# Loading the values and output weights of a decode kernel's full-cache part from Pool's software DMA queue

## The chip, the cores, the metric

One Trainium2 chip, one core. The time is the device time of one execution in microseconds (us), as the median of several executions. "Span" is the length of the one profiled execution, which is 1.7 to 1.9 us shorter than its time. PE is the matmul engine (TensorE), DVE is VectorE, ACT ScalarE, Pool GpSimd, SP SyncE.

## The reference

Two attention decode steps, their outputs side by side: part A has a sliding window and 4 query heads per key head, part B has 32 heads over a full cache of 8192 positions. Batch 4, one query position, bfloat16.

```python
def _B_ref(x, k_cache, v_cache, wq, wo):           # A: the last 2048 positions, 8 key heads
    B, Sq, D = x.shape                             # 4, 1, 512
    H, Dh = 32, 128
    q = (x @ wq).reshape(B, Sq, H, Dh).transpose(0, 2, 1, 3)
    scores = jnp.einsum("bhqd,bhkd->bhqk", q, k_cache) * (Dh ** -0.5)
    p = softmax(scores)
    o = jnp.einsum("bhqk,bhkd->bhqd", p, v_cache)
    return o.transpose(0, 2, 1, 3).reshape(B, Sq, H * Dh) @ wo
return jnp.concatenate([a, b], axis=-1)
```

The caches of B alone are 2 x 268 MB, each byte used once. It is a kernel of loads.

## The kernel before

Part B is cut into 64 chunks: two heads of one batch element each. A chunk has 4 MB of keys and 4 MB of values (128 partitions, one row of 32 KB in each). On PE, the keys are transposed tile by tile and multiplied with the query ("keys"); the values of the chunk before are multiplied with its probabilities in between ("values"). Two buffers of keys and two of values; every fourth chunk 256 KB of output weights, in one buffer. I call the chunks of B 0 to 63.

All loads are issued by SP, in one line, in the order of their use: keys c+1, values c, keys c+2, ...

```python
def dma_wos(hp):                                   # output weights, waits until their reader is done
    src = B_wo[2 * hp * P:2 * (hp + 1) * P, :].rearrange("(p r) n -> p (r n)", r=2)
    sch.add_dma("sp", lambda e: e.dma_start(wos[...], src), "d_wos",
                waits=[("fin", NCA + 4 * hp - 1)] if hp else [], key=("wos", hp))

def dma_kv(kind, c):
    ...                                            # waits: the last reader of the buffer (transposes or products)
    if kind == "v" and c == NC - 1:                # last values: five pieces, 64, 32, 16, 8, 8 tiles
        for i, n in enumerate(LASTV):
            sch.add_dma("sp", lambda e, x=x: e.dma_start(dst[:, x], src[:, x]), "d_vl%d" % i, ...)
        return
    if kind == "k" and c == NC - 1:                # last keys: 96 tiles (24 KB rows), then 32 (8 KB rows)
        sch.add_dma("sp", lambda e: e.dma_start(dst[:, x[0]], src[:, x[0]]), "d_h%d" % at, ...)
        sch.add_dma("sp", lambda e: e.dma_start(dst[:, x[1]], src[:, x[1]]), "d_kl", key="kl")
        return
    sch.add_dma("sp", lambda e: e.dma_start(dst, src), "d_h%d" % at, waits=waits, key=(kind, c))

for kind, c in loads:                              # k0 k1 v0 k2 v1 ...
    if kind == "k" and c >= NCA and (c == NCA or (c - NCA) % 4 == 3 and c > NCA + 3):
        dma_wos((c - NCA) // 4)
    dma_kv(kind, c)
    ...
```

On PE, for each chunk c: `keys_part(c)`, 16 groups of 8 transposes and 8 score products, then `values_part(c - 1, c)`.

Of the kernel before, what the change touches and what calls it, by code (L numbers as in the profile page):

```python
# [11 lines left out]

P = 128
TG = 8
NTRB = 3
NKT = 4
NH = 10
NWO = 3
# [141 lines left out]
def bass_concat_heads__sliding_block_cached__mha_block_cached__decode_kernel(  # L160
# [30 lines left out]
    NC = len(chunks)  # L191
    NCA = Hkv
    groups = []
    for c, ch in enumerate(chunks):
        ch["UC"] = ch["U"] * ch["C"]
        assert ch["NT"] % TG == 0 and ch["NT"] * P * 2 <= (1 if ch["ab"] == 0 else 2) * 16384
        ch["NG"] = ch["NT"] // TG
        ch["s"] = len(groups)
# [5 lines left out]
    NONE = -1  # L204
    sch = _Sched()
    with ExitStack() as es:
        block = es.enter_context(nc.Block())

        def sb(name, shape, dt):
            return es.enter_context(nc.sbuf_tensor(name, shape, dt))  # L210

        def ps(name, shape, dt):
            return es.enter_context(nc.psum_tensor(name, shape, dt))

        kv = sb("kv", [P, NH, 8192], BF16)
        kt = sb("kt", [P, NKT, TG * P], BF16)
        wos = sb("wos", [P, 2, DO], BF16)
# [31 lines left out]
        wol = sb("wol", [P, 2, DO], BF16)  # L249
        tr = ps("tr", [P, NTRB, TG * P], BF16)  # L250
        sc = ps("sc", [P, 2, 512], F32)
        po = ps("po", [P, 512], F32)
        ms = ps("ms", [P, 512], F32)
        fin = ps("fin", [P, 512], F32)
        xtps = ms[:, XT0:XT0 + KC * NB].bitcast(BF16)

        semnames = ["eng_pe", "eng_dve", "eng_act", "eng_pool", "eng_sp", "d_x0", "d_x1", "d_o0", "d_o1"]
        semnames += ["d_h%d" % i for i in range(NH)] + ["d_vl%d" % i for i in range(len(LASTV))]
        semnames += ["d_wo%d" % i for i in range(NWO)] + ["d_wos", "d_kl"]
        sems = {n: es.enter_context(nc.semaphore(n)) for n in semnames}  # L260


# [42 lines left out]
        def take(load, at, n, release):  # L305
            waits = []
            for i in range(at, at + n):
                waits += held[i]
                held[i] = [release]
            half_of[load] = at  # L310
            return waits

        def flat(at, n):
            return kv[:, at:at + n, :].rearrange("p s x -> p (s x)")
# [10 lines left out]
        def wo_slot(g):  # L325
            return g % 2 if g < NCA - 1 else 2

        def dma_wo(g):

            src = A_wo[g * 4 * P:(g + 1) * 4 * P, :].rearrange("(p r) n -> p (r n)", r=4)  # L330
            slot = wo_slot(g)
            dst = wor[:, slot, :]
            sch.add_dma("sp", lambda e: e.dma_start(dst, src), "d_wo%d" % slot,
                        waits=[("fin", g - 2)] if g >= 2 and slot < 2 else [], key=("wo", g))

        def dma_wos(hp):


            src = B_wo[2 * hp * P:2 * (hp + 1) * P, :].rearrange("(p r) n -> p (r n)", r=2)
            sch.add_dma("sp", lambda e: e.dma_start(wos[:, :, :].rearrange("p r n -> p (r n)"), src), "d_wos",  # L340
                        waits=[("fin", NCA + 4 * hp - 1)] if hp else [], key=("wos", hp))

        def dma_kv(kind, c):
            ch = chunks[c]
            T = {("k", 0): A_k, ("k", 1): B_k, ("v", 0): A_v, ("v", 1): B_v}[(kind, ch["ab"])]

            at = HALF_A[kind][c % 2] if ch["ab"] == 0 else (0 if kind == "k" else 4) + 2 * (c % 2)

            if kind == "v" and c == NC - 1:
                at = 8  # L350
            waits = take((kind, c), at, 1 if ch["ab"] == 0 else 2, ("T", ch["s_last"]) if kind == "k" else ("pv", c))
            if kind == "v" and c == NCA + 1:
                waits = waits + [("pv", NONE)]
            if ch["ab"] == 0:
                src = T[:, ch["g"], SkA - W:, :].rearrange("b (pp j) d -> pp b (j d)", pp=P // NB)
                sch.add_dma("sp", lambda e: e.dma_start(kv[:, at, :], src), "d_h%d" % at, waits=waits, key=(kind, c))
                return
            src = T[ch["b"], 2 * ch["hp"]:2 * ch["hp"] + 2].rearrange("u (pp j) d -> (u pp) (j d)", pp=P // 2)
            dst = flat(at, 2)
            if kind == "v" and c == NC - 1:  # L360

                j0 = 0
                for i, n in enumerate(LASTV):
                    x = slice(j0 * P, (j0 + n) * P)
                    sch.add_dma("sp", lambda e, x=x: e.dma_start(dst[:, x], src[:, x]), "d_vl%d" % i, waits=waits, key=("vl", j0))  # L365
                    j0 += n
                return
            if kind == "k" and c == NC - 1:

                x = slice(0, LASTK * P), slice(LASTK * P, NTB * P)  # L370
                sch.add_dma("sp", lambda e: e.dma_start(dst[:, x[0]], src[:, x[0]]), "d_h%d" % at, waits=waits, key=(kind, c))
                sch.add_dma("sp", lambda e: e.dma_start(dst[:, x[1]], src[:, x[1]]), "d_kl", key="kl")
                return
            sch.add_dma("sp", lambda e: e.dma_start(dst, src), "d_h%d" % at, waits=waits, key=(kind, c))

        dma_x(0)
        dma_x(1)
# [7 lines left out]
        loads.remove(("v", NCA - 1))  # L385
        loads.insert(loads.index(("k", NCA)), ("v", NCA - 1))
        for kind, c in loads:
            if kind == "k" and c >= NCA and (c == NCA or (c - NCA) % 4 == 3 and c > NCA + 3):
                dma_wos((c - NCA) // 4)
            dma_kv(kind, c)  # L390
            if kind == "v" and c > NCA and (c - NCA) % 2 == 1:


                hp = max(0, c - NCA - 2) // 4
                sch.add("sp", lambda e: e.sem_inc(sems["eng_sp"], 1), waits=[("wos", hp)] + (["kl"] if c == NC - 1 else []),
                        key=("wos2", c - 2 if c > NCA + 1 else NONE), self_inc=True)
            if kind == "v" and c < NCA:
                dma_wo(c)
        sch.add("sp", lambda e: e.sem_inc(sems["eng_sp"], 1), waits=[("wos", HB // 2 - 1)], key=("wos2", NC - 1), self_inc=True)


# [4 lines left out]
        def pe_mm(o, l, r, start=True, stop=True, transpose=False, waits=(), key=None):  # L406
            if transpose:
                sch.add("pe", lambda e: e.transpose(o, l, r), waits, key)  # L408
            else:
                sch.add("pe", lambda e: e.matmul(o, l, r, start=start, stop=stop), waits, key)  # L410
# [41 lines left out]
        def ahead(c, n):  # L452

            return c - n if c - n >= NCA else NONE

        bank_used = [None] * NTRB

        def emit_T(s):
            c, g = groups[s]
            bank = g % NTRB  # L460
            if c == NCA and g == 0:
                bank_used[:] = [None] * NTRB
            before, bank_used[bank] = bank_used[bank], s
            for t in range(TG):
                waits = []
                if t == 0:
                    waits = [("k", c), "c_identb"] if g == 0 else []
                    waits += [("ev", before)] if before is not None else []
                    if c >= NCA and c % 2 == 1 and g == LASTK // TG:
                        waits += [("wos2", ahead(c, 2))]  # L470
                pe_mm(tr[:, bank, t * P:(t + 1) * P], tile_of("k", c, g * TG + t), identb[:, :], transpose=True,
                      waits=waits, key=("T", s) if t == TG - 1 else None)
            src, dst = tr[:, bank, :], kt[:, s % NKT, :]
            waits = [("T", s)] + ([("S", s - NKT)] if s >= NKT else [])
            if (g % 3 == 2) if c >= NCA else (g in (0, 1, 3, 5)):
                sch.add("act", lambda e: e.activation(dst, src, ACTF.Copy), waits=waits, key=("ev", s))  # L476
            else:
                sch.add("dve", lambda e: e.tensor_copy(dst, src), waits=waits, key=("ev", s))  # L478
# [268 lines left out]
        def keys_part(c):  # L747
            ch = chunks[c]
            if c % 2 == 0:
                sch.mark()  # L750
            for g in range(ch["NG"]):
                emit_T(ch["s"] + g)
                if g >= SLAG:
                    emit_S(ch["s"] + g - SLAG)

                for what in A_ORDER.get(g, []) if c < NCA else []:
                    do_A(what, c)
                if c >= NCA and c % 2 == 0 and g == 6:
                    norm_sum(ahead(c, 1))
                if c >= NCA and c % 2 == 1 and g == 8:  # L760
                    emit_sel(ahead(c, 2))
                if c >= NCA and c % 2 == 1 and g == 10:
                    emit_fin(ahead(c, 2))
# [117 lines left out]
```

## Time and profile before

| | before |
|---|---|
| time, median | 1374.2 us |
| bytes read | 587.2 MB, 428 GB/s over the span |
| DMA engines, share of the span in packets | 99.8% |
| PE busy | 86% |
| last landing, then to the end of the span | 1369.1 us, 3.5 us |

The page has one digit per fortieth of the span for each engine (tenths of busy time), and a GB/s row below. A load's "us to landing" counts from its issue, so it includes the wait behind earlier loads of its queue. The lines stand in the prediction.

### The profile page before, as it was taken

How to read it: one execution, taken by the hardware profiler on the slowest of the kernel's cores; microseconds unless marked ns; L12 is line 12 of the kernel's file. 1: busy time of each engine (PE TensorE's matmuls, PEld its weight loads, DVE VectorE, ACT ScalarE, POOL GpSimd, SP SyncE). 2: the span in 40 equal slices, each digit the busy share in tenths (PEclk: the TensorE clock that was granted, in tenths of full speed). 3: DMA queues.
4: the chain of work that ended last, by engine and by line, in shares of the span. 5: the costliest groups of instructions: out<-in, count | busy, mean ns of one | idle time of the engine just before them, and what ended most of it. 6: DMA issues, size and time to landing. Idle time of an engine off the chain costs nothing.

```text
span 1372.6 us, 59967 instructions
## 1 busy us (share of the span) xinstructions
PE 1176.5 (86%) x27065; PEld 1132.9 (83%) x27067; DVE 656.6 (48%) x1434; ACT 434.7 (32%) x650; POOL 7.3 (1%) x28
## 2 busy tenths in 40 slices
PE   4888898889888888988888888888898888888888
PEld 4777898888888888888888878888898888888888
DVE  1775454445444444454445444444454444444544
ACT  1553232333223322332233323322333233323322
POOL 2000000000000000000000000000000000000000
PEclk9998999999999999999999999999999999999999
DMA  9999999999999999999999999999999999999998
GB/s 400 423 424 432 429 433 428 433 432 432 432 431 433 429 434 428 434 430 434 430 434 430 430 433 432 432 431 433 429 433 431 434 429 434 430 432 432 432 427 352
DMA packets 25261, 587.53 MB, mean 428 GB/s; under 512 B 2820, under 2 KB 2840, under 8 KB 6296
## 3 DMA queue, kind: packets, MB, share of 16 engines
q1 hardware_dynamic: 25208, 587.22, 99.8%
q8 instruction: 16, 0.26, 0.1%
q14 instruction: 5, 0.04, 0.0%
q10 hardware_dynamic: 32, 0.01, 0.0%
HBM read 587.21 MB, written 0.01 MB: 428 GB/s over the span
## 4 chain that ended last, share of the span: by engine, by line
DMA 65%; PE 33%; issue 1%; DVE 1%; ACT 0%; SPq 0%; DVEq 0%
DMA kv<-in_B_k_cache_dram 57%; PE tr L408 21%; PE sc L410 9%; DMA kv<-in_A_k_cache_dram 5%; DMA kv<-in_B_v_cache_dram 3%; PE po L410 2%; PE fin L410 1%; PE ms L410 0%; ACT kt L476 0%; DVE sA L527 0%; SPq L365 0%; ACT pba L597 0%; PE ms L408 0%; DVE zA L683 0%; DVE rm L536 0%
## 5 line engine op out<-in xcount | busy, mean ns | idle before, releaser
L408 PE MATMUL tr<-identb,kv 128*128 128x128 bf16 x8704 | 697.9, 230 | 148.8 <-DMA kv<-in_B_k_cache_dram 141.5
L478 DVE COPY kt<-tr 128x1024 bf16<-128x1024 bf16 x736 | 502.6, 690 | 457.1 <-PE tr L408 452.7
L408 PEld LDWEIGHTS tr<-identb,kv 128*128 128x128 bf16 x8704 | 552.9, 104 | 165.2 <-DMA kv<-in_B_k_cache_dram 81.7
L476 ACT ACTIVATE kt<-tr 128x1024 bf16<-128x1024 bf16 x352 | 359.3, 1023 | 666.8 <-PE tr L408 666.7
L410 PE MATMUL sc<-qb,kt 128*128 128x64 bf16 x8704 | 446.2, 196 | 14.3 <-ACT kt L476 12.8
L410 PEld LDWEIGHTS sc<-qb,kt 128*128 128x128 bf16 x8704 | 366.4, 100 | 26.0 <-ACT kt L476 20.2
L410 PE MATMUL po<-pbb,kv 128*128 128x64 bf16 x8320 | 284.4, 192 | 4.5 <-issue 3.9
L410 PEld LDWEIGHTS po<-pbb,kv 128*128 128x128 bf16 x8320 | 263.2, 97 | 7.1 <-issue 4.1
L577 ACT ACTIVATE pbb<-sc,negb 64x128 bf16<-64x128 f32 x128 | 51.6, 403 | 254.3 <-DVE negb L564 253.5
L541 DVE TENSOR_REDUCE rm<-sc 64x1 f32<-64x128 f32 x128 | 37.0, 289 | 56.6 <-PE sc L410 55.7
L553 DVE TENSOR_REDUCE gm<-ms 1x2 f32<-1x128 f32 (+1 forms) x72 | 20.1, 279 | 48.4 <-PE ms L408 48.4
L564 DVE COPY negb<-ms 128x1 f32<-128x1 f32 (+1 forms) x72 | 11.4, 158 | 47.0 <-PE ms L410 46.8
L410 PE MATMUL ms<-identf,gx 1*128 1x1 f32 (+1 forms) x144 | 27.2, 256 | 0.8 <-DVE zA L683 0.8
L666 DVE TENSOR_TENSOR oz<-po,rz 128x8 bf16<-128x8 f32 x33 | 5.5, 166 | 40.7 <-PE po L410 40.7
L410 PEld LDWEIGHTS ms<-identf,gx 1*128 1x128 f32 (+1 forms) x144 | 21.1, 182 | 4.6 <-DVE zA L683 0.9
L577 ACT ACTIVATION_READ_ACCUMULATOR pbb<-sc,negb 64x1 f32 x128 | 23.7, 185 | 0.0
L410 PE MATMUL po<-pba,kv 128*128 128x64 bf16 x512 | 20.5, 199 | 3.5 <-issue 2.1
L410 PEld LDWEIGHTS po<-pba,kv 128*128 128x128 bf16 x512 | 17.9, 102 | 5.7 <-ACT pba L597 4.2
L408 PE MATMUL ms<-identf,rm 128*1 128x128 f32 (+1 forms) x72 | 19.5, 271 | 2.4 <-DVE rm L536 2.3
L557 DVE TENSOR_SCALAR gx<-gm 1x128 f32<-1x128 f32 (+1 forms) x72 | 16.0, 222 | 2.5
L683 DVE CAST zB<-ms 64x8 bf16<-64x8 f32 x64 | 10.5, 164 | 9.2 <-PE ms L410 8.7
L410 PE MATMUL ms<-xT,kv 128*128 128x4 bf16 x256 | 7.1, 166 | 8.8 <-DMA kv<-in_A_wq_dram 5.0
(61 smaller groups left out, 173.9 us busy)
## 6 DMA issues: line engine op xcount, KB each, us to landing
kv<-in_B_k_cache_dram SPq DMA_DIRECT2D x63, 4096.0 KB, 26.5
kv<-in_B_v_cache_dram SPq DMA_DIRECT2D x63, 4096.0 KB, 30.9
kv<-in_A_k_cache_dram SPq DMA_DIRECT2D x8, 2048.0 KB, 14.8
kv<-in_A_v_cache_dram SPq DMA_DIRECT2D x8, 2048.0 KB, 16.2
kv<-in_A_wq_dram SPq DMA_DIRECT2D x1, 4096.0 KB, 12.5
kv<-in_B_wq_dram SPq DMA_DIRECT2D x1, 4096.0 KB, 27.1
wor<-in_A_wo_dram SPq DMA_DIRECT2D x8, 512.0 KB, 9.8
wos<-in_B_wo_dram SPq DMA_DIRECT2D x16, 256.0 KB, 20.3
```

Of the source, the lines that this page charges most:

```text
L408: sch.add("pe", lambda e: e.transpose(o, l, r), waits, key)
L410: sch.add("pe", lambda e: e.matmul(o, l, r, start=start, stop=stop), waits, key)
L476: sch.add("act", lambda e: e.activation(dst, src, ACTF.Copy), waits=waits, key=("ev", s))
L478: sch.add("dve", lambda e: e.tensor_copy(dst, src), waits=waits, key=("ev", s))
L541: sch.add("dve", lambda e, src=src, pp=pp: e.tensor_reduce(out=rm[pp, m, 0:1], in_=src, axis=AX.X, op=ALU.max), waits=[("S", ch["s_last"]) ...
L553: sch.add("dve", lambda e: e.tensor_reduce(out=gm[0:C, m, 0:U], in_=src, axis=AX.X, op=ALU.max), waits=[("trm", c)], key=("gmax", c))
L557: sch.add("dve", lambda e: e.tensor_scalar(out=dst, in0=gv, scalar1=-scale, scalar2=None, op0=ALU.mult), waits=[("gmax", c)], key=("gx", c))
L564: sch.add("dve", lambda e: e.tensor_copy(negb[:, m, 0:C], ms[:, col:col + C]), waits=[("bc", c)], key=("negb", c))
L577: sch.add("act", lambda e, src=src, pp=pp, n=n, u=u: e.activation(probs_of(c)[pp, :, u], src, ACTF.Exp, bias=negb[pp, m, 0:1], scale=scale ...
L666: sch.add("dve", lambda e: e.tensor_tensor(out=o, in0=i0, in1=i1, op=ALU.mult), waits=waits, key=("oT", c))
L683: sch.add("dve", lambda e, src=src, pp=pp: e.tensor_copy(z[pp, :].rearrange("p (r b) -> p r b", r=k), src), waits=[("sm", c)] + free if h ...
```

## The change

Intent: take the values and the output weights off SP's line, so that keys and values, whose buffers come free at different moments, wait apart and not in one line. Pool had nothing to do after the first 10 us.

```diff
+VQ = "pool"
 ...
 def dma_wo(g):                                    # sliding part
+    if slot == 2:
+        sch.add_dma(VQ, lambda e: e.dma_start(dst, src), "d_p6", waits=[("k", g)], key=("wo", g))
+        return
 ...
 def dma_wos(hp):
-    sch.add_dma("sp", ..., "d_wos",
+    sch.add_dma(VQ if hp else "sp", ..., "d_ws" if hp else "d_wos",
                 waits=[("fin", NCA + 4 * hp - 1)] if hp else [], key=("wos", hp))
 ...
+    if kind == "v" and c == NCA:                  # the first values: after ten groups of the first keys
+        waits = waits + [("T", ch["s"] + 10)]
 ...
-            sch.add_dma("sp", lambda e, x=x: e.dma_start(dst[:, x], src[:, x]), "d_vl%d" % i, ...)
+            sch.add_dma(VQ, lambda e, x=x: e.dma_start(dst[:, x], src[:, x]), "d_vl%d" % i, ...)
 ...
-    sch.add_dma("sp", lambda e: e.dma_start(dst, src), "d_h%d" % at, waits=waits, key=(kind, c))
+    sch.add_dma("sp" if kind == "k" else VQ, lambda e: e.dma_start(dst, src),
+                ("d_h%d" if kind == "k" else "d_p%d") % at, waits=waits, key=(kind, c))
+
+def dma_values(c):                                # the order on Pool
+    if c > NCA + 3 and (c - NCA) % 4 == 1:
+        dma_wos((c - NCA) // 4)
+    dma_kv("v", c)
```

(Cut: SP's signal that the weights have landed moves behind the keys; new semaphores; the lines that call `dma_values` among PE's instructions, eleven groups into a chunk's keys, two in the last chunk.)

More of the change, by code (lines that the diff above doesn't have):

```diff
@@ L258, in bass_concat_heads__sliding_block_cached__mha_block_cached__decode_kernel @@
         semnames += ["d_h%d" % i for i in range(NH)] + ["d_vl%d" % i for i in range(len(LASTV))]
-        semnames += ["d_wo%d" % i for i in range(NWO)] + ["d_wos", "d_kl"]
+        semnames += ["d_wo%d" % i for i in range(NWO)] + ["d_wos", "d_kl", "d_ws", "d_p4", "d_p6"]
         sems = {n: es.enter_context(nc.semaphore(n)) for n in semnames}
@@ L332, in dma_wo @@
             dst = wor[:, slot, :]
+            if slot == 2:
+                sch.add_dma(VQ, lambda e: e.dma_start(dst, src), "d_p6", waits=[("k", g)], key=("wo", g))
+                return
             sch.add_dma("sp", lambda e: e.dma_start(dst, src), "d_wo%d" % slot,
-                        waits=[("fin", g - 2)] if g >= 2 and slot < 2 else [], key=("wo", g))
+                        waits=[("fin", g - 2)] if g >= 2 else [], key=("wo", g))
         def dma_wos(hp):
             src = B_wo[2 * hp * P:2 * (hp + 1) * P, :].rearrange("(p r) n -> p (r n)", r=2)
-            sch.add_dma("sp", lambda e: e.dma_start(wos[:, :, :].rearrange("p r n -> p (r n)"), src), "d_wos",
+            sch.add_dma(VQ if hp else "sp", lambda e: e.dma_start(wos[:, :, :].rearrange("p r n -> p (r n)"), src), "d_ws" if hp else "d_wos",
                         waits=[("fin", NCA + 4 * hp - 1)] if hp else [], key=("wos", hp))
@@ L364, in dma_kv @@
                     x = slice(j0 * P, (j0 + n) * P)
-                    sch.add_dma("sp", lambda e, x=x: e.dma_start(dst[:, x], src[:, x]), "d_vl%d" % i, waits=waits, key=("vl", j0))
+                    sch.add_dma(VQ, lambda e, x=x: e.dma_start(dst[:, x], src[:, x]), "d_vl%d" % i, waits=waits, key=("vl", j0))
                     j0 += n
@@ L373, in dma_kv, with say_landed @@
                 return
-            sch.add_dma("sp", lambda e: e.dma_start(dst, src), "d_h%d" % at, waits=waits, key=(kind, c))
+            sch.add_dma("sp" if kind == "k" else VQ, lambda e: e.dma_start(dst, src), ("d_h%d" if kind == "k" else "d_p%d") % at, waits=waits, key=(kind, c))
+        def dma_values(c):
+            if c > NCA + 3 and (c - NCA) % 4 == 1:
+                dma_wos((c - NCA) // 4)
+            dma_kv("v", c)
+        def say_landed(c):
+            hp = max(0, c - NCA - 2) // 4
+            sch.add("sp", lambda e: e.sem_inc(sems["eng_sp"], 1), waits=[("wos", hp)] + (["kl"] if c == NC - 1 else []),
+                    key=("wos2", c - 2 if c > NCA + 1 else NONE), self_inc=True)
         dma_x(0)
@@ L387, in bass_concat_heads__sliding_block_cached__mha_block_cached__decode_kernel @@
         for kind, c in loads:
-            if kind == "k" and c >= NCA and (c == NCA or (c - NCA) % 4 == 3 and c > NCA + 3):
-                dma_wos((c - NCA) // 4)
-            dma_kv(kind, c)
-            if kind == "v" and c > NCA and (c - NCA) % 2 == 1:
-                hp = max(0, c - NCA - 2) // 4
-                sch.add("sp", lambda e: e.sem_inc(sems["eng_sp"], 1), waits=[("wos", hp)] + (["kl"] if c == NC - 1 else []),
-                        key=("wos2", c - 2 if c > NCA + 1 else NONE), self_inc=True)
+            if kind == "k" and c == NCA:
+                dma_wos(0)
+            if kind == "k" or c < NCA:
+                dma_kv(kind, c)
+            if kind == "k" and c > NCA + 1 and (c - NCA) % 2 == 0:
+                say_landed(c - 1)
             if kind == "v" and c < NCA:
                 dma_wo(c)
+        say_landed(NC - 1)
         sch.add("sp", lambda e: e.sem_inc(sems["eng_sp"], 1), waits=[("wos", HB // 2 - 1)], key=("wos2", NC - 1), self_inc=True)
@@ L751, in keys_part @@
             for g in range(ch["NG"]):
+                if c >= NCA and g == (11 if c < NC - 1 else 2):
+                    dma_values(c)
                 emit_T(ch["s"] + g)
```

## The prediction

> **What bounds the kernel now.** I read the page first (slices, queues, landings), then the chain of waits, the waits of all engines, the stretches, and last the timeline of the end. From the page's slices:
>
> ```profile
> PE   4888898889888888988888888888898888888888
> DMA  9999999999999999999999999999999999999998
> GB/s 400 423 424 432 429 433 428 433 432 432 432 431 433 429 434 428 434 430 434 430 434 430 430 433 432 432 431 433 429 433 431 434 429 434 430 432 432 432 427 352
> ```
>
> Each figure is a fortieth of the span (34.3 us). The DMA row is full in every slice but the last; no slice moves over 434 GB/s. PE is never full for long. The page's parts on queues and issues:
>
> ```profile
> q1 hardware_dynamic: 25208, 587.22, 99.8%
> ...
> kv<-in_B_k_cache_dram SPq DMA_DIRECT2D x63, 4096.0 KB, 26.5
> kv<-in_B_v_cache_dram SPq DMA_DIRECT2D x63, 4096.0 KB, 30.9
> ...
> wos<-in_B_wo_dram SPq DMA_DIRECT2D x16, 256.0 KB, 20.3
> ```
>
> One queue carries all 587 MB, and its packets take 99.8% of what 16 engines have: 0.2% of 1372.6 us is about 3 us of idling in the whole run. A 4096 KB load alone would take 4.194 MB / 431 GB/s = 9.7 us, but lands 26.5 us (keys) or 30.9 us (values) after its issue, so it finds 17 or 21 us of work queued ahead of it. That is the second thing to see: loads are issued long before the queue would run dry. The stretches show it for the full-cache part (columns: stretch, length, busy of PE, its weight loads, DVE, ACT, Pool, then PE clock, DMA share, GB/s):
>
> ```profile
> 160.00:1320.00 1160.00, 1006.83 (x23320) 977.98 (x23317) 550.87 (x1164) 360.16 (x539) 0.00 (x0) 0.94 1.00 431
> ```
>
> DMA share 1.00 over 1160 us at 431 GB/s; Pool does nothing, so it is free to issue. The waits say the same from the other side:
>
> ```profile
> SPq L374 <- PE sc L410: 687.5, 61, 16.5
> SPq L374 <- PE po L410: 333.0, 63, 18.3
> SPq L340 <- PE fin L410: 165.7, 15, 13.3
> ...
> PE tr L408 <- DMA kv<-in_B_k_cache_dram: 141.5, 58, 4.1
> ...
> PE po L410 <- DMA kv<-in_B_v_cache_dram: 0.7, 2, 0.5
> ```
>
> SP waits over 1100 us for buffers to come free, yet the rings stay full meanwhile, so those waits cost nothing. PE waits for keys (141.5 us, 2.4 us each time), hardly ever for values. The end, in the chain:
>
> ```profile
> 1329.92 39.14 DMA kv<-in_B_v_cache_dram
> 1369.11 0.42 PE po L410 x8
> 1369.84 0.40 PE fin L410 x4
> 1370.27 0.42 DVE outB L724
> ```
>
> The last slice of values lands at 1369.1 us and 3.5 us of work follow. So the time is: sum of all DMA packets (about 1369 us) plus 3.5 us. Only the packets' own duration, a dry queue, or the few us after the last landing can move it.
>
> **What the Trainium skill says.** (1) "DMA: Bandwidth & Descriptors", section "Issuing engines are not separate DMA queues": DMAs of SP, ACT and GpSimd run on the same 16 engines and interleave; another issuer saves only issue time. The trace agrees that issue is no cost: 0.33 us on SP per 4 MB load. (2) The same page, "SWDGE vs HWDGE vs iDMA": on Pool's path software writes descriptors into rings in SBUF, and an engine round-robins between the two kinds of queue at packet boundaries, a packet being preferably at most 4096 B. The kernel before has no data on that path, so how its descriptors are cut is not shown here. (3) "SBUF — State Buffer", "Who interferes with whom": a DVE copy in a 2-port mode locks Pool out of SBUF, and with it the descriptor writing. (4) "VectorE: DVE Perf Modes", "Why PSUM operands drop a tier": a PSUM operand excludes the 2-port modes. The big DVE copies here (736 of 690 ns) read PSUM, so Pool should not be locked out for long; no run shows it yet.
>
> **The change part by part.**
> - Removed from SP: 64 chunks of values (68 DMAs, the last chunk in five pieces), 15 of 16 loads of output weights, at 0.33 us of issue each, about 28 us, none on the path.
> - Added on Pool: those 83 DMAs and one 512 KB load of sliding-part weights. A Pool issue may cost more than SP's 0.33 us, say 1 to 2 us; with 17 to 21 us queued ahead, that is hidden.
> - Bytes, order within each kind, buffers (two for keys, two for values), and the programs of PE, DVE and ACT stay; the order of instructions differs there only in the semaphores waited for.
> - Moved: keys and values no longer stand in one line. They share the engines, each about 215 GB/s while both have work, so a load takes about 19.5 us of service instead of 9.7, starting earlier. One chunk of keys and values is 8.39 MB, at 431 GB/s 19.5 us; PE needs 12.5 us for keys (chain: 1271.04 to 1283.5) and 5.3 us for values (the next two issues on SP, 1283.50 and 1288.85), 17.8 us. PE is the faster side by 1.7 us, so it can only stop while some buffer is still being loaded, and the engines have work then. Steady state: 0 us.
> - Values wait behind output weights on Pool. In the timeline such a weight load is issued 3.3 us before the next keys (1241.88 against 1245.15), the values they now precede 5.35 us after the keys before. With a chunk of 19.7 us those values go out 19.7 - 5.35 - 3.3 = 11 us later, every fourth chunk. 21 us of work stood ahead of them, so 10 us of margin remain: 0 us.
> - The start of the full-cache part: the first values now wait for group 10 of the first keys' transposes, about when the second keys land. One gap of 0 to 2 us.
> - The end: before, the last keys had only one chunk of values ahead of them. Now, at 1327.3 (when the last values are issued) some 1 MB of the keys before and 4.2 MB of the last keys share with three chunks of values: 5.2 MB / 215 GB/s = 24 us against (1 + 4 + 4.2) / 431 = 21 us. The last keys land some 3 us later. PE then needs 12.5 + 5.3 us, then 128 products of the last values (about 5 us with the weights' unpacking) and 3.5 us. Before, PE and the last landing finished together (PE waited only 0.35 us for the last slice); so 0 to +3 us.
> Sum without any change in packet cost: 1374.2 + about 2 = 1376 us.
>
> **The rivals.**
> - Dearer packets. The packet records of the trace average 1218 ns for 32 KB, 620 for 16 KB, 161 for 4 KB, 84.6 for 2 KB. Values are 8192 packets of 32 KB. If Pool's path cuts them to 16 KB: 8192 x 22 / 16 = +11 us. To 4 KB: 8192 x (1291 - 1218) / 16 = +37 us, 1411 us. To 2 KB: +69 us. Against it: the descriptor is shaped by the row, 32 KB contiguous on both sides. I give a cut to 4 KB or less 6%. Ring reads from SBUF could slow single engines a little too; with 512 packets per engine, 10 ns each is 5 us.
> - Cheaper packets. If two rings hide the fixed part between packets (1213 ns is the least seen for 32 KB, 1218 the mean; a line through 16 and 32 KB gives about 9 ns fixed), 5 to 10 us may be won: 1364 to 1369. More is not to be had: 587.21 MB at the best slice's 434 GB/s are 1353 us, still only 1.5% below. Over 2% needs 437 GB/s throughout, which no slice shows.
> - Keys become late and PE the bound. PE's waits for keys may grow from 141.5 us, and waits for values appear; neither costs time while the DMA row stays full. For it to cost, both queues must run dry, at the delayed values: 15 times 2 us would be 30 us. The 10 us margin speaks against it; 4%.
> - A gain from taking apart SP's line: SP's waits look large, but keys are released before values in each chunk, the order in which SP issues, so no free buffer is kept waiting. Nothing to win.
>
> **Range and chances.** 1376 us as the middle: saturated engines, a few us at the end. Down 10 for cheaper packets, up 14 for a 16 KB cut or a slower engine: 1366 to 1390. Faster by over 2%: 1%. Slower by over 2%: 7% (small packets or dry queues). Within 2%: 92%.
>
> **What would show it.** Right: a second queue on the page with about 272 MB and near half of the packet time; 428 GB/s give or take 3 over the span; DMA row full; landings of keys and values both different from 26.5 and 30.9 but no lower rate; the SP row of waits for products (333 us) gone; the last landing within a few us of 1369. Step by step wrong: more packets than 25,261 by thousands (a cut); slices with a DMA digit under 9 in the full-cache part (dry queues); over 6 us between the last landing and the end (the end's PE work). The prediction fails if GB/s in the middle leaves 425 to 435.

## The result

| | before | after |
|---|---|---|
| time, median (range) | 1374.2 us (1374.04 to 1374.27) | 1380.8 us (1380.56 to 1381.57) |
| ratio | | 1.0049, 95% interval 1.0032 to 1.0067 |
| span profiled | 1372.6 us | 1379.8 us |

A ratio is the mean time of one kernel's fast runs over that of the other's in the same rounds, so not quite the ratio of the medians. The result is within 2% and inside the stated range; it is also clear of noise, half a per cent slower. Where do the 7.2 us of the spans come from? The page of the changed kernel, slices, queues and issues:

```profile
DMA  9999999999999999999999999999999999999996
GB/s 400 422 425 407 426 435 428 432 431 428 437 430 432 430 428 433 432 432 432 429 433 427 431 436 431 430 427 433 434 430 433 431 429 431 429 436 431 430 429 285
...
q1 hardware_dynamic: 13112, 314.32, 53.1%
q0 software_dynamic: 11008, 272.90, 46.1%
...
kv<-in_B_k_cache_dram SPq DMA_DIRECT2D x63, 4096.0 KB, 23.6
kv<-in_B_v_cache_dram POOLq DMA_DIRECT2D x63, 4096.0 KB, 29.7
```

The two queues share the packet time almost evenly, and the slices read as before except in two places: the fourth (407 instead of 432) and the last (285 instead of 352). The stretches of both kernels put numbers to that. Before:

```profile
100.00:160.00 60.00, 49.84 (x1024) 44.71 (x1025) 30.93 (x80) 19.14 (x28) 0.00 (x0) 0.89 1.01 430
```

After:

```profile
100.00:160.00 60.00, 46.92 (x922) 42.13 (x923) 29.06 (x75) 19.15 (x28) 1.76 (x3) 0.88 0.99 415
160.00:1320.00 1160.00, 997.64 (x23341) 964.10 (x23339) 548.22 (x1164) 358.72 (x537) 38.71 (x73) 0.93 1.00 431
```

The long middle moves 431 GB/s in both. The hand-over from A to B (100 to 160 us) loses 15 GB/s, and the packet records show the engines idle for 1.3 us near 132 us, where the first values of B now wait for ten groups of the first keys. I call this wait the gate. PE's waits have changed sides: for keys 141.5 us before and 22.2 now, for values 0.7 us before and 134.2 now:

```profile
PE po L427 <- DMA kv<-in_B_v_cache_dram: 134.2, 36, 9.4
...
PE tr L425 <- DMA kv<-in_B_k_cache_dram: 22.2, 14, 2.4
```

In the middle that costs nothing, as the engines stay full. At the end it does. The timeline of PE near the end of the kernel before (start, length, engine, line, work, and in brackets the idle time before it and what ended it); rows with `tr<-` and x24 open a chunk's keys, rows with `po<-` and x16 a chunk's values:

```profile
1342.27 0.64 PE L410 MATMUL po<-pbb,kv 128*128 128x64 bf16 x16
1347.01 1.51 PE L408 MATMUL tr<-identb,kv 128*128 128x128 bf16 x24
1359.21 0.64 PE L410 MATMUL po<-pbb,kv 128*128 128x64 bf16 x16 [0.46 <-DMA kv<-in_B_v_cache_dram]
```

These are values 61, keys 63 and values 62. The same three after:

```profile
1348.95 1.03 PE L427 MATMUL po<-pbb,kv 128*128 128x64 bf16 x16 [4.60 <-DMA kv<-in_B_v_cache_dram]
1355.60 1.50 PE L425 MATMUL tr<-identb,kv 128*128 128x128 bf16 x24
1367.16 0.64 PE L427 MATMUL po<-pbb,kv 128*128 128x64 bf16 x16
```

PE waits for values 61 until 1348.95, and starts the last keys 8.6 us later than before; from there it waits for no load to the end. Of the 8.6 us, 6.7 are the later start of values 61. The other 1.9 are their products, 6.65 us long instead of 4.74. The views of these two stretches show TensorE's granted clock (the third figure from the end) at full speed before:

```profile
1342.20:1347.00 4.80, 4.74 (x147) 4.54 (x143) 1.37 (x7) 0.91 (x4) 0.00 (x0) 1.00 1.01 430
```

and at 0.64 after:

```profile
1348.90:1355.60 6.70, 6.65 (x139) 6.53 (x140) 1.23 (x5) 0.88 (x4) 0.00 (x0) 0.64 1.03 439
```

Why the clock was lower there, no run tests. The last loads themselves land at about 1370.4 us (issued at 1335.8, 34.6 us to landing), only 1.3 us later than before. So the end grew from 3.5 us after the last landing to 9.4: about 6 us are PE's (some 1.9 of them the slower products), about 1.3 us the loads'. One reason why values 61 are late is in Pool's timeline, with the output weights in the first row:

```profile
1322.50 0.54 POOL L344 DMA_DIRECT2D wos<-in_B_wo_dram  x1 [25.12 <-PE fin L427]
1323.03 0.53 POOL L380 DMA_DIRECT2D kv<-in_B_v_cache_dram  x1
1333.16 0.53 POOL L380 DMA_DIRECT2D kv<-in_B_v_cache_dram  x1 [9.60 <-PE po L427]
```

Their buffer was free when the products of chunk 59 were done, near 1313, but Pool stood at the weights until 1322.5.

### The profile page after: what moved, and what is told of

Its sections match the earlier page's. It is cut to its first block, busy times and chain, and to the rows that moved or that the text cites. A ratio compares the mean times of both kernels' runs of the same rounds, so it can differ in the third digit from the quotient of the medians.

```text
span 1379.8 us, 59935 instructions
## 1 busy us (share of the span) xinstructions
PE 1167.7 (85%) x27065; PEld 1120.2 (81%) x27067; DVE 654.0 (47%) x1434; ACT 435.2 (32%) x650; POOL 52.1 (4%) x112
## 4 chain that ended last, share of the span: by engine, by line
DMA 62%; PE 35%; issue 1%; DVE 1%; POOL 1%; ACT 0%; SPq 0%; DVEq 0%
DMA kv<-in_B_v_cache_dram 35%; DMA kv<-in_B_k_cache_dram 22%; PE tr L425 16%; PE po L427 9%; PE sc L427 7%; DMA kv<-in_A_k_cache_dram 3%; DMA kv<-in_B_wq_dram 2%; PE ms L427 1%; PE fin L427 1%; POOL wos L344 1%; PE ms L425 0%; ACT kt L493 0%; DVE sA L544 0%; ACT pba L614 0%; DVE zA L700 0%
## 5 line engine op out<-in xcount | busy, mean ns | idle before, releaser
L425 PE MATMUL tr<-identb,kv 128*128 128x128 bf16 x8704 | 652.5, 221 | 32.1 <-DMA kv<-in_B_k_cache_dram 22.2
L425 PEld LDWEIGHTS tr<-identb,kv 128*128 128x128 bf16 x8704 | 511.8, 99 | 46.6 <-DMA kv<-in_B_k_cache_dram 21.9
L427 PE MATMUL sc<-qb,kt 128*128 128x64 bf16 x8704 | 438.7, 194 | 15.3 <-ACT kt L493 12.8
L427 PE MATMUL po<-pbb,kv 128*128 128x64 bf16 x8320 | 321.1, 201 | 137.4 <-DMA kv<-in_B_v_cache_dram 134.2
L427 PEld LDWEIGHTS po<-pbb,kv 128*128 128x128 bf16 x8320 | 298.2, 103 | 144.8 <-DMA kv<-in_B_v_cache_dram 138.5
L427 PEld LDWEIGHTS sc<-qb,kt 128*128 128x128 bf16 x8704 | 356.3, 99 | 27.5 <-ACT kt L493 20.2
L380 POOL DMA_DIRECT2D kv<-in_B_v_cache_dram x63 | 33.4, 530 | 804.2 <-PE po L427 774.0
L344 POOL DMA_DIRECT2D wos<-in_B_wo_dram x15 | 8.1, 543 | 386.8 <-PE fin L427 386.8
```

What stands on the lines that cost most here:

```text
L344: sch.add_dma(VQ if hp else "sp", lambda e: e.dma_start(wos[:, :, :].rearrange("p r n -> p (r n)"), src), "d_ws" if hp else "d_wos", waits ...
L380: sch.add_dma("sp" if kind == "k" else VQ, lambda e: e.dma_start(dst, src), ("d_h%d" if kind == "k" else "d_p%d") % at, waits=waits, key=( ...
L425: sch.add("pe", lambda e: e.transpose(o, l, r), waits, key)
L427: sch.add("pe", lambda e: e.matmul(o, l, r, start=start, stop=stop), waits, key)
```

## The experiments

Theories at the outset: (1) the weights in front of values 61 make PE late; (2) the last keys come late, as they take turns with values; (3) the software queue is slower in itself. Theory 4, made after the first four runs: one line serves loads in the order of their use, two lines serve late-needed bytes beside early-needed ones. Each run had five timed rounds beside the kernel before (1374.1 to 1374.2 in each group; `one_pool_line` gave four times). The three groups ran on three different chips, so a difference of 1 or 2 us between runs of different groups is less sure than the ranges say.

### weights_after_values

```diff
 def dma_values(c):
-    if c > NCA + 3 and (c - NCA) % 4 == 1:
-        dma_wos((c - NCA) // 4)
     dma_kv("v", c)
+    if c > NCA + 3 and (c - NCA) % 4 == 1:
+        dma_wos((c - NCA) // 4)
```

> Only the order of two issues on Pool is changed: in each fourth chunk the values are issued first, the output weights after them. Theory 1 (the end is late because the weights stand in front of the last-but-two values, which then wait about 11 us for the weights' buffer and 10 us more while 8 small weight packets per engine take turns with 1.22 us key packets): those values land about 10 us earlier, the last keys' transposes start near 1347 instead of 1355.8, time 1373.5 to 1376. Theory 2 (the last keys themselves land too late, the 8 KB slice at 1358.9): the keys still hold the end up, 1378 to 1381. Theory 3 (the software queue is slower in itself): 1380 to 1381.

Measured: 1379.19 us (1377.66 to 1381.27), ratio to before 1.0038. Keys 62, values 61 and keys 63 in PE's timeline:

```profile
1335.21 2.36 PE L427 MATMUL tr<-identb,kv 128*128 128x128 bf16 x24 [2.06 <-DMA kv<-in_B_k_cache_dram]
1348.07 0.64 PE L429 MATMUL po<-pbb,kv 128*128 128x64 bf16 x16
1352.58 1.50 PE L427 MATMUL tr<-identb,kv 128*128 128x128 bf16 x24
```

PE no longer waits for values 61. But keys 62 now started at 1335.2, after 2.06 us of waiting for their load, so the last keys gain only 3 us. The time fell by 1.6 us, less than expected, and the times of the two versions overlap: the order on Pool is a part of the cause, not the whole. PE's waits for values did not go, they moved: 133.9 us in total here, 134.2 in the changed kernel. In this run a long one (7.2 us, until 1295.1) is for the values that now stand right behind the weights; near the end only values 62 stand there, and they land at 1361.4, before PE comes to them at 1364.5. The packet records also show the engines idle for 2.3 us at the hand-over from A to B, 1.0 us more than in the changed kernel.

### weights_on_sp

```diff
-    sch.add_dma(VQ if hp else "sp", ... wos ...)
+    sch.add_dma("sp", ... wos ...)               # and issued in front of the keys, as in the kernel before
```

> Values stay on Pool, the output weights go back to SP, at the place they had before the change. If only the wait on Pool in front of the values costs (Theory 1 without the packet turns): 1373.5 to 1376. If the engines take turns packet by packet whatever a packet's size (Theory 1 with the turns): the weights' 2 KB packets now hold up the last keys behind them by about 8 x (1.22 + 0.085) = 10 us, and the time stays at 1378 to 1382. Landing of a weight load near 10 us or more in both cases. Theory 3: 1380 to 1381.

Measured: 1389.26 us (1388.88 to 1396.92), ratio 1.0121; with `one_pool_line` the slowest version. No values wait behind weights here, so the theory that this wait is all that costs falls. The weights' small packets now hold up keys. The last keys' two parts in the profiled run, issues and landings:

```profile
kv<-in_B_k_cache_dram SPq DMA_DIRECT2D x1, 3072.0 KB, 31.6
...
kv<-in_B_k_cache_dram SPq DMA_DIRECT2D x1, 1024.0 KB, 37.2
```

The first part takes 31.6 us where the changed kernel needs 21.2. That is 10.4 us more, the size that 8 rounds of a 2 KB packet beside a 1.22 us one give; the cost to the time was larger than I expected. It does not lie at the end alone: from 160 to 1320 us this run moved 429 GB/s instead of 431, which is some 5 us, and PE waited 179.6 us for keys (22.2 in the changed kernel). The times lie in two groups, 1389 and 1396; why, I don't know.

### whole_last_keys

```diff
-    if kind == "k" and c == NC - 1:              # two parts, 24 KB and 8 KB rows
+    if kind == "k" and c == NC:                  # never: one load, 32 KB rows
```

> The last keys are loaded in one piece with 32 KB packets, not in 24 KB and 8 KB packets. By turns of packets the two pieces need 8 x (1.22 + 0.92) + 8 x (1.22 + 0.31) = 29 us beside 32 KB packets of values (the trace shows 33.0 us to the landing of the second), one piece 8 x 2.44 = 19.5 us: the last keys land some 8 to 10 us earlier, near 1350. Theory 2 (they hold up the end): time 1373 to 1377. Theory 1 (PE comes to them only at 1355.8, because of the late values): no gain, 1379 to 1381.5.

Measured: 1384.02 us (1383.51 to 1384.64), ratio 1.0073: 3 us slower than the changed kernel. The edit did what it should: the last keys landed at 1348.7, where the second part had landed at 1358.9. Theory 2 falls; the last keys are not what the end waits for. Values 61 and keys 63:

```profile
1351.19 1.03 PE L427 MATMUL po<-pbb,kv 128*128 128x64 bf16 x16 [5.10 <-DMA kv<-in_B_v_cache_dram]
1357.55 1.50 PE L425 MATMUL tr<-identb,kv 128*128 128x128 bf16 x24
```

Values 61, which share the engines with the last keys, land 2.2 us later. The packet records account for most of it: up to that landing each engine served eight 32 KB packets of the last keys (8 x 1.22 us), in the changed kernel eight of 24 KB and two or three of 8 KB (8 x 0.92 + 2.6 x 0.31), which is an estimate of 1.6 us. Keys 62 had also landed 0.4 us later, before the edit had any effect.

### one_pool_line

The kernel before, with keys, values and weights of B all on Pool in the old single order (first version).

```diff
-sch.add_dma("sp", ...)                            # keys, values, weights of B
+sch.add_dma("pool", ...)                          # own semaphores, as Pool's queue needs them at 0
```

> The kernel before with all loads of the full-cache part, keys too, on Pool's software queue in the old single order. Theory 3 (the software queue is slower, by 0.53 us issues, descriptors or packets): 1378 or more. Theories 1 and 2 (only the sharing between two lines costs): 1374 to 1376, 431 GB/s in the middle, 32 KB packets near 1.218 us, and 3.5 us from the last landing to the end.

Measured: 1389.46 us (1388.08 to 1391.52), ratio 1.0115. Read alone, this speaks for theory 3. The page's GB/s row says where:

```profile
GB/s 400 425 423 377 384 352 433 430 430 431 436 430 427 435 431 430 431 433 431 433 431 431 432 431 430 431 434 431 429 431 435 429 431 434 431 431 431 431 429 357
```

Three slices at the hand-over from A to B, and nothing after them. My edit had done that: B's first loads ran beside A's last ones, and PE's first pair of chunks fell out of its loop (at 174 us PE stood 6.2 us for no reason in the profile). The run settles nothing; it was repeated below.

### end_in_order

```diff
+    if kind == "v" and c == NC - 2:
+        waits = waits + [("k", NC - 1)]          # values 62 and 63: after the first part of the last keys
 def dma_values(c):                                # and weights after values, as above
```

> Weights after values on Pool, and the last two chunks of values are held back until the first part of the last keys has landed, so that they take no turns from the keys that PE needs first. Theory 4 (the kernel before ends early because its single line serves the loads in the order of their use; with two lines the bytes that are needed last are served beside those needed first, and PE, which has some 26 us of work from the start of the last keys, starts them at 1352 to 1356 instead of 1347): the last keys start 3 to 5 us earlier than in the run with weights after values, time 1374 to 1377. Rival (PE is behind for what happened earlier, or the held-back loads leave the engines dry): 1378 to 1382.

Measured: 1376.98 us (1376.49 to 1377.90), ratio 1.0022: 2.2 us below the run without the hold. The last keys start at 1350.2 instead of 1352.6. Keys 62, values 61 and keys 63:

```profile
1334.20 1.51 PE L429 MATMUL tr<-identb,kv 128*128 128x128 bf16 x24 [1.44 <-DMA kv<-in_B_k_cache_dram]
1345.71 0.65 PE L431 MATMUL po<-pbb,kv 128*128 128x64 bf16 x16
1350.22 1.50 PE L429 MATMUL tr<-identb,kv 128*128 128x128 bf16 x24
```

The last piece lands at about 1370.9 (issued at 1351.0, 19.9 us to landing) and the span ends at 1374.7, 3.8 us later: the last landing and PE's work now end together, though from 1334.2 on the chain of waits holds no load.

Does this show theory 4? The profiles do not. Of the 2.4 us, 1.0 was there when keys 62 started, and their load was issued before the hold had any effect (in this run the engines idled 0.9 us at the hand-over, 2.3 in the other). The other 1.4 us lie between keys 62 and values 61, where PE waited for no load in either run; the granted clock there was 0.87 without the hold and 1.00 with it. What the hold itself saved PE is 0.3 us, a wait for SP's signal that the second part of the last keys had landed. The medians of five times do differ by 2.2 us, but the two groups ran on different chips. Theory 4 stays not shown as the cause of the late end.

What this run does show is the turns by themselves. The second part of the last keys, 1 MB in 8 KB packets, after (beside 32 KB packets of values) and here (values held back); "us to landing" of the first part and of the second, which is issued 0.37 us later. After:

```profile
kv<-in_B_k_cache_dram SPq DMA_DIRECT2D x1, 3072.0 KB, 21.2
...
kv<-in_B_k_cache_dram SPq DMA_DIRECT2D x1, 1024.0 KB, 33.0
```

Here:

```profile
kv<-in_B_k_cache_dram SPq DMA_DIRECT2D x1, 3072.0 KB, 21.1
...
kv<-in_B_k_cache_dram SPq DMA_DIRECT2D x1, 1024.0 KB, 23.4
```

33.0 + 0.37 - 21.2 = 12.2 us against 23.4 + 0.37 - 21.1 = 2.7 us for the same bytes. Each engine has 8 such packets; 8 x (1.22 + 0.31) = 12.2 us with one packet of values between each two, where 1.22 us is a 32 KB packet and 0.31 us an 8 KB packet in the records. Two queues share the engines by packets, not by bytes.

### end_in_order_no_gate

```diff
-        waits = waits + [("T", ch["s"] + 10)]    # the first values wait no longer for the first keys' groups
```

> The same, and the first values of the full-cache part no longer wait for ten groups of the first keys. The 1.3 to 2.3 us in which the engines run dry near 131 us should go, and with them that much of the end if the end is bound by the loads: 1 to 2 us below the run with the end in order, 1373 to 1375. If that start is not on the path, no difference; if those values now take turns from the second keys and delay PE, slower by 1 to 3 us.

Measured: 1375.48 us (1374.80 to 1376.27), ratio 1.0011 with an interval of 0.9997 to 1.0025, so not told apart from the kernel before. It is 1.5 us below the run with the gate, as expected.

### one_pool_line2

```diff
+# the last values of A and the weights after them are on Pool too, in front of B's: the old order at the
+# hand-over; one semaphore is counted up early, so PE's loops are those of the kernel before
```

> A cleaner version of the single line on Pool: the hand-over from SP keeps the old order and the loops of PE are those of the kernel before. If the 14 us of the first version came from the hand-over (slices 4 to 6 at 377, 384 and 352 GB/s, 431 after them), now 1374 to 1377. If the software queue itself costs (Theory 3): 1384 or more, with the middle slices below 428 GB/s or the end longer than 3.5 us after the last landing.

Measured: 1374.35 us (1374.19 to 1375.14), ratio 1.0003, interval 0.9990 to 1.0017: equal to the kernel before. Its queue and its GB/s row:

```profile
GB/s 402 422 425 433 426 434 428 434 433 431 432 429 435 428 434 430 433 431 432 432 431 433 427 436 428 435 429 434 430 432 432 428 436 428 435 429 435 429 427 355
...
q0 software_dynamic: 20592, 543.70, 92.2%
```

With 92% of the packet time on the software queue, nothing is lost. Theory 3 falls.

### smaller_weight_packets

```diff
-    sch.add_dma(VQ ..., wos[128 x 1024] <- src ...)
+    for x in (slice(0, DO), slice(DO, 2 * DO)):
+        sch.add_dma(VQ ..., wos[:, x] <- src[:, x] ...)
```

> The changed kernel with each weight load on Pool cut into two of half the columns: the same bytes in twice as many packets of half the size. Turns of packets (a weight packet waits for one 1.22 us packet of keys each time): a weight load takes 16 x (1.22 + 0.045) = 20 us instead of 10.4, the values behind it land up to 10 us later, and the time rises by 5 to 10 us to 1386 to 1391. If only the bytes or the 11 us of waiting count: 1380 to 1382.

Measured: 1382.86 us (1382.12 to 1384.74), ratio 1.0068. The test failed at its premise: the packets did not get smaller. The records have the same 1344 packets of 4 KB on Pool's queue in this run as in the changed kernel, 64 for each 256 KB of weights; only the completion packets are more. Pool's queue had joined the weights' 2 KB rows in pairs all along, and joined the 1 KB rows in fours here. (SP's queue does not: 128 packets of 2 KB for the same load.) So a weight load on Pool took four turns on each engine, not the eight that I had expected for `weights_after_values`. What the 2 us come from, I leave open; each weight load has one more issue of 0.54 us in front of the values.

### no_gate

```diff
-        waits = waits + [("T", ch["s"] + 10)]    # in the changed kernel, alone
```

> The changed kernel without the wait of the first full-cache values for ten groups of the first keys. If the 1.3 us of dry engines near 131 us lie on the path to the end: 1379 to 1380. If PE's path alone sets the end, whatever the start: 1380.5 to 1381.5. Slice 4 of the page back to about 430 GB/s in both cases.

Measured: 1380.19 us (1379.78 to 1380.83), ratio 1.0044. The fourth slice is back at 430 GB/s and the last keys start at 1354.32, 1.3 us earlier than in the changed kernel. In time it is 0.6 us, near the noise between groups of runs; together with the 1.5 us above I count the gate as about 1 us.

### hold_last_values

```diff
+    if kind == "v" and c == NC - 2:
+        waits = waits + [("k", NC - 1)]          # in the changed kernel, alone
```

> The changed kernel with only the last two chunks of values held back until the first part of the last keys has landed; the weights stay in front of the last-but-two values. Theory 1 (those last-but-two values, landing at 1349, are what PE waits for at the end): holding back what comes behind them on the same queue can't bring them forward, 1379.5 to 1382. Theory 4 in its plain form (any late-needed byte served early costs): 1376 to 1379. The second part of the last keys lands within 3 to 8 us of the first instead of 12, as it loses its company.

Measured: 1381.26 us (1380.98 to 1382.07), ratio 1.0051: no gain, although the second part of the last keys now lands 4.5 us after the first instead of 12.2. Values 61 and keys 63:

```profile
1349.44 0.64 PE L429 MATMUL po<-pbb,kv 128*128 128x64 bf16 x16 [3.07 <-DMA kv<-in_B_v_cache_dram]
1355.52 1.50 PE L427 MATMUL tr<-identb,kv 128*128 128x128 bf16 x24
```

Values 61 still come at 1349. What stands behind them on their queue is not their trouble; by the runs above, the weights in front and the keys beside them are. Theory 4 in its plain form, that any late-needed byte served early costs, had forecast 1376 to 1379 here and falls.

### All runs in one table

| run | time, us | start of the last keys, us | span | span minus start |
|---|---|---|---|---|
| before | 1374.2 | 1347.0 | 1372.6 | 25.6 |
| after | 1380.8 | 1355.6 | 1379.8 | 24.2 |
| weights_after_values | 1379.2 | 1352.6 | 1377.2 | 24.6 |
| weights_on_sp | 1389.3 | 1368.1 | 1395.1 | 27.0 |
| whole_last_keys | 1384.0 | 1357.6 | 1381.8 | 24.2 |
| end_in_order | 1377.0 | 1350.2 | 1374.7 | 24.5 |
| end_in_order_no_gate | 1375.5 | 1348.7 | 1373.1 | 24.4 |
| one_pool_line2 | 1374.4 | 1346.8 | 1372.3 | 25.5 |
| smaller_weight_packets | 1382.9 | 1356.2 | 1380.4 | 24.2 |
| no_gate | 1380.2 | 1354.3 | 1378.5 | 24.2 |
| hold_last_values | 1381.3 | 1355.5 | 1379.7 | 24.2 |

In the two-line versions the end is 24.2 to 24.6 us after PE starts the last keys (27 in weights_on_sp, where the second part of the last keys was late too; its profiled run is one of the slower group): PE's own work sets it. In the two single-line versions PE starts so early that it waits for the last loads, 25.5 us. No experiment points to a version that beats the kernel before: the packets alone fill its span to 3 us, and 3.5 us of work must follow the last landing.

## Why the prediction was right, and where it was off

**Saturated engines, 0 us in the middle: right.** 431 GB/s over the 1160 us in both kernels, packets of 32 KB at 1.219 us on either queue (1.218 before), all values uncut. The rivals of dearer and cheaper packets both failed, and the long waits of SP that vanished were worth nothing.

**Pool's issues hidden: right.** 0.53 us each against 0.33 on SP; one_pool_line2 is the direct proof. DVE's large copies have the same mean as before (691 against 690 ns) and no Pool issue of a 4 MB load took over 0.54 us, so a lock between the two did not show.

**The start, one gap of 0 to 2 us: right.** 1.3 us of idle engines; removing the gate gave 0.6 and 1.5 us in two pairs of runs.

**"Values wait behind output weights", 0 us: right in the middle, though not by the margin; wrong at the end.** The late issue was about right: 11 us forecast, 9.6 measured for values 61 (1313.4 to 1323.0). The 10 us of margin were not there: PE waited 3.3 to 9.4 us for values after each of the 15 weight loads on Pool. In the middle that cost nothing because the engines stayed full, as the prediction's rival of late keys says. For values 61 there is no later chunk to hide it: PE gets them at 1348.95, 4.6 us late. Weights first or values first is worth 1.6 us alone, with overlapping times.

**The end, 0 to +3 us: the term that was mis-sized.** It measured about +6 us, some 1.9 of them slower products at a lower granted clock, of which the prediction says nothing. The step counted on sharing by bytes ("each about 215 GB/s while both have work"). The engines share by packets, so the last keys' 8 KB packets ran at a fifth of the rate, and they landed 12.2 us after the first part. That the last keys would be what PE waits for was wrong too: holding their company back, or loading them whole, didn't help; the late ones were values 61. So the sharing that the step got wrong is shown, but the late second part of the keys is not what delayed PE. With the weights put behind the values, the last two loads held back and the gate gone, the time is within 1.3 us of the kernel before. What those 1.3 us are is open, and the interval includes none; nor is it shown how much each of the three edits gave, as the hold alone gave nothing.

**A slip in the rivals.** The 620 ns for 16 KB mixes in 16 packets of another queue (1047 ns each); without them the mean is 616, and the cut to 16 KB would have cost 7 us, not 11. The "9 ns fixed" follow from the least packets (611 and 1213 ns), not from the means beside them, which give 22. Neither rival came true, so nothing hung on it.

**Net.** 1376 was expected and 1380.8 measured, inside 1366 to 1390: the middle carried the prediction, and the 4.8 us of error lie mostly in the end.

## What to carry to other kernels

When one queue keeps the DMA engines full and its order is the order of use, a second queue added no bandwidth here; it changed who waits. Look at the two ends, where no later load hides a late one, and count the shares of two queues by packets: small rows beside large ones got a small share (12.2 us for 1 MB instead of 2.7), so keep rows alike on queues that run together. Put loads on a queue in the order in which their buffers come free; here that was worth some 1.6 us. When two profiles differ by a few us, look where the difference begins, and at the granted clock, before you credit the edit.

## What the Trainium skill lacked or had wrong

- "DMA: Bandwidth & Descriptors", section "SWDGE vs HWDGE vs iDMA", says that an engine goes round between the queues at packet boundaries, but not what follows for their shares. Here 1 MB in 8 KB packets took 12.2 us beside 32 KB packets of the other queue and 2.7 us without them. It also puts a packet on Pool's path at preferably at most 4096 B. Here that held for joining small rows (2 KB rows in 4 KB packets, 64 for 256 KB), not for cutting large ones: rows of 32 KB went as single packets, 1.219 us each, as on SP's queue.
- The same page, section "Issuing engines are not separate DMA queues", says that issuing from several engines only saves issue time. For bandwidth the runs agree (431 GB/s either way); what it lacks is that loads then land in another order: PE's waits moved from keys (141.5 us) to values (134.2 us), and the changed kernel, its gate at the start included, was 6.6 us slower.
- The same page, section "Issuing engine by pattern", calls the path of SP and ACT generally faster. For 4 MB loads queued ahead, Pool's single line was equal (ratio 1.0003).
